# Chunked linear attention ahead of a gated matmul layer: from half-array matmuls on 128-token chunks to quarter-array matmuls on 64-token halves

## The chip, the cores and the metric

The kernel runs on one core of one Trainium2 chip. The metric is the device time of one execution in microseconds (us); smaller is better. Each kernel was run several times, and the medians below say of how many runs. "First output matmul" will mean the start of the first matmul that multiplies with `w_out`. It splits a run into a *start*, in which attention for the first four blocks has to wait for loads, and a *steady part*.

Engines are named as in the profile: PE is TensorE (matmuls), PEld its weight loads, DVE is VectorE, ACT is ScalarE, POOL is GpSimd (which in this kernel also issues most loads), SP is SyncE.

## The reference

```python
# q, k, v: (4 batches, 8 heads, 768 tokens, 64), float32
gamma = 1.0 - 2.0 ** (-5.0 - np.arange(8))
state = 0
for t in range(768):
    state = gamma * state + outer(k[t], v[t])          # per batch and head, 64x64
    y[t]  = (1/8) * q[t] @ state
x = y with the heads side by side                       # (3072, 512)
h = x @ w_in                                            # w_in (512, 2048)
out = (h * cos(h)) @ w_out                              # w_out (2048, 512), out (3072, 512)
```

The kernel works in bf16 with float32 accumulation. It removes gamma by scaling q with gamma^t/8 and k·v with gamma^-t, so that the recurrence becomes plain chunked attention: inside a chunk a masked score matrix (A) times V, plus q times the state at the start of the chunk; then the state grows by the chunk's K^T V.

## The kernel before

A "pair" is one chunk of 128 tokens of two batches, so there are 12 pairs, and two pairs make one group `g` of 512 columns of X. There are three attention stages per pair: scores and masks, Y (with the copy to X), and the state update. Around them TensorE does dense 128x128 matmuls: `unit_f` and `pair_f` multiply X with `w_in`, `unit_o` the activated result with `w_out`.

```python
# A: 16 matmuls, contraction 64, so two run side by side on the two row halves
def stage_a(p):
    for b in range(2):
        for a in range(HP):                 # HP = 4 couples of heads
            for j in range(2):              # head 2a+j
                nc.tensor.matmul(ap[j][:, a, :], lhsT=kt(n, b, a)[64*j : 64*j + 64, :],
                                 rhs=qt(n, b, a)[64*j : 64*j + 64, :], tile_position=(64*j, 0))
# Y: 32 matmuls with 64 output rows, two side by side on the column halves
def stage_yb(p, b):
    for a in range(HP):
        if c > 0:
            for j in range(2):              # q times state; stb holds zeros beside each 64x64 state
                nc.tensor.matmul(yp[ts(j, 64), a, :], lhsT=stb[p % 2][:, b, a, ts(j, 64)],
                                 rhs=qt(n, b, a), start=True, stop=False, ...)
        for j in range(2):                  # masked scores times V
            nc.tensor.matmul(yp[ts(j, 64), a, :], lhsT=vs[n][:, b, 2*a + j, :],
                             rhs=am[p % 2][b][j][:, a, :], ...)
    nc.scalar.copy(out=xt[(p // 2) % 2][:, :, ts(2 * (p % 2) + b, C)], in_=yp)
# S: 16 matmuls of 128x64, accumulated in one PSUM bank over all chunks of a batch
def stage_s(p, copy_st): ...
```

In the timeline of the kernel before, the two matmuls of a couple in A and in Y start 3 to 4 ns apart, and the next couple 56 ns after the first: about the time of 128 columns of one dense matmul (0.216 us for 512, so 54 ns). In that sense two run side by side.

A load of a part of `w_in` is one instruction on POOL. The part of the start that this text is about reads so (cuts marked by "..."):

```python
load(nc.gpsimd, 1, ("q0", "q1", "k0", "k1"))
load_w_in(0, 256); load_w_in(1, 256)
conv_q(1, nc.gpsimd)                         # POOL scales q of pair 1
load(nc.gpsimd, 1, ("v0", "v1")); load_w_in(1)
load(nc.gpsimd, 2, ("q0", "q1", "k0", "k1"))
conv_v(1, nc.gpsimd)                         # POOL scales v of pair 1
...
m1 = stage_a(1); masks(1, m1); pair_f(0, 0, (1,), later); ...
stage_y(1, nc.scalar.copy)                   # Y of both batches (each copied to X at once), then the state
pair_f(1, 0); pair_f(0, 1)                   # pair_f(p, r): r-th quarter of X(p) @ w_in
conv_q(2, nc.vector); conv_k(2, True); pair_f(1, 1); stage_t(2, None); ...
```

## Time and profile before

Before the change the median was 219.63 us of 3 runs (219.62 to 220.47).

| | before |
|---|---|
| span of the profiled run | 218.3 us |
| TensorE busy | 206.5 us, 95% |
| first output matmul | 58.09 us |
| from there to the end | 160.2 us |
| attention of one pair in the steady part, on TensorE | 2.0 us |

These lines are from the page of the kernel before. The first gives busy time, share of the span and number of instructions per engine; the next three are tenths of busy time in 40 slices of 5.5 us (PEclk is the clock that TensorE was granted, 9 being 90% or more); the last is the chain of waits that ended last, by engine.

```profile
PE 206.5 (95%) x1725; PEld 114.0 (52%) x1725; DVE 113.2 (52%) x183; ACT 118.4 (54%) x187; POOL 99.0 (45%) x113
...
PE   7986999989999999999999999999999999999993
...
POOL 7999999959999984729042070000000000000000
PEclk9999999999999999999999999999999999999999
...
PE 80%; POOL 9%; DVE 4%; ACT 4%; issue 2%; DVEq 0%; POOLq 0%; ACTq 0%
```

TensorE is the bound: from slice 10 to the last but one it is at 90% or more throughout. In the first fourteen slices POOL works with one gap, in slice 9, and it is the second engine of the chain of waits (9%). The granted clock is full in every slice of the row. But the trace has a record of the clock only from 6.54 us on; the ten dummy matmuls before, from 1.26 to 5.50 us, took 0.42 us each, twice the 0.216 us that a matmul of this size takes later. The same in microseconds, from the windows view of the kernel before (window, length, then busy time and number of instructions of PE, PEld, DVE, ACT, POOL; granted clock; DMA share; GB/s):

```profile
0.00:20.00 20.00, 16.11 (x143) 8.90 (x143) 12.35 (x29) 11.31 (x17) 18.82 (x27) 1.00 0.93 209
20.00:40.00 20.00, 18.10 (x244) 15.27 (x245) 14.12 (x23) 14.47 (x24) 19.87 (x24) 1.00 1.13 261
40.00:58.10 18.10, 16.62 (x206) 14.48 (x204) 13.65 (x22) 13.44 (x22) 15.72 (x18) 1.00 0.94 244
...
78.00:200.00 122.00, 122.00 (x866) 58.39 (x865) 64.25 (x97) 64.79 (x103) 24.76 (x26) 1.00 0.46 106
```

From 78 to 200 us TensorE never idles, and DVE and ACT are busy a little over half of the time. The waits view of the kernel before, TensorE from 8 us to the first output matmul (who waits for whom; us in total, times, longest):

```profile
PE bank_67 L234 <- POOL vs_119 L156: 1.6, 1, 1.6
...
PE bank_68 L292 <- ACT xt_135 L238: 0.5, 1, 0.5
PE bank_63 L292 <- ACT xt_134 L238: 0.4, 1, 0.4
...
PE bank_69 L234 <- POOL vs_119 L156: 0.4, 1, 0.4
```

All waits of that list, with those left out here, sum to 5.9 us. The longest is for `vs_119`, V of pair 1, which POOL scales. Waits for X (`xt`) after a Y stage are short, 0.4 to 0.5 us.

One Y stage with its state update, from the timeline of TensorE in the steady part (start, duration, engine, line, operation, output<-inputs, sizes, count):

```profile
137.58 1.03 PE L305 MATMUL bank_65<-w_out_sb,gt_136 128*128 128x512 bf16 x4
138.53 0.25 PE L229 MATMUL bank_64<-qkt_121,stb_133 128*64 128x128 bf16 x2
...
139.80 1.04 PE L281 MATMUL bank_66<-xt_135,w_in_sb 128*128 128x512 bf16 x4
```

Durations overlap (the page lists a dense matmul of 512 columns with 379 ns, while in the timeline they start 0.216 us apart), so starts are what to compare. Four dense matmuls of 512 columns take 0.86 us (0.216 each), so those that start at 137.58 are done at 138.45; the next dense one starts at 139.80. Y and the state cost 1.35 us, and A, in another place, 0.65: 2.0 us per pair. Each change between full and half array costs about 0.09 us of that, and there are four.

The first output matmul, from the same view of the start:

```profile
58.09 3.62 PE L305 MATMUL bank_66<-w_out_sb,gt_136 128*128 128x512 bf16 x16
```

### The profile page before, as it was taken

To read this page: it belongs to the slowest core of one execution; us is meant where nothing else is said; L and a number is where in the kernel's file an instruction comes from. 1 tells how busy PE (TensorE), PEld (TensorE's weight loads), DVE (VectorE), ACT (ScalarE), POOL (GpSimd) and SP (SyncE) were. 2 spreads that over 40 slices of the span, in tenths; PEclk is the share of its full clock that TensorE was granted. 3 is DMA by queue.
4 is the path that set the end of the run, shared out by engine and by line. 5 is a ranking of instruction groups with operands and counts; after the bars stand their busy time and mean duration, and the time that the engine had idled before them with its cause. 6 is when DMAs were issued, how large, how long until landed. Compare 5 with 4: busy or idle time off the path is not lost.

```text
span 218.3 us, 4318 instructions
## 1 busy us (share of the span) xinstructions
PE 206.5 (95%) x1725; PEld 114.0 (52%) x1725; DVE 113.2 (52%) x183; ACT 118.4 (54%) x187; POOL 99.0 (45%) x113
## 2 busy tenths in 40 slices
PE   7986999989999999999999999999999999999993
PEld 2554877968756454544544544544544544444441
DVE  4486496795714516557448537547647244433000
ACT  7365857848854656556456555555534634444120
POOL 7999999959999984729042070000000000000000
PEclk9999999999999999999999999999999999999999
DMA  6999999999476999792991942613511011110212
GB/s 156 324 161 235 264 282 236 203 305 332 116 241 164 291 223 290 182 296 54 182 250 55 158 127 82 66 48 99 51 48 51 0 48 48 51 48 2 96 62 82
DMA packets 44084, 32.78 MB, mean 150 GB/s; under 512 B 32800, under 2 KB 37664, under 8 KB 44064
## 3 DMA queue, kind: packets, MB, share of 16 engines
q0 software_dynamic: 9072, 18.35, 33.4%
q1 hardware_dynamic: 34848, 14.03, 27.6%
q8 instruction: 13, 0.21, 0.4%
q10 hardware_dynamic: 144, 0.13, 0.2%
q14 instruction: 7, 0.06, 0.1%
HBM read 27.26 MB, written 6.29 MB: 154 GB/s over the span
## 4 chain that ended last, share of the span: by engine, by line
PE 80%; POOL 9%; DVE 4%; ACT 4%; issue 2%; DVEq 0%; POOLq 0%; ACTq 0%
PE bank_65 L305 10%; PE bank_63 L281 9%; PE bank_67 L305 8%; PE bank_68 L305 6%; PE bank_66 L305 6%; PE bank_64 L281 5%; PE bank_69 L281 4%; PE bank_69 L305 4%; PE bank_66 L281 4%; PE bank_67 L281 3%; PE bank_63 L292 2%; PE bank_64 L292 2%; PE bank_63 L305 2%; PE bank_64 L305 2%; POOL qs_113 L151 1%
## 5 line engine op out<-in xcount | busy, mean ns | idle before, releaser
L281 PEld LDWEIGHTS <-w_in_sb 128*128 128x128 bf16 x256 | 24.1, 98 | 28.3
L305 PEld LDWEIGHTS <-gt_137 128*128 128x128 bf16 x192 | 18.8, 98 | 22.7
L305 PEld LDWEIGHTS <-gt_136 128*128 128x128 bf16 x192 | 18.5, 98 | 21.6
L292 PEld LDWEIGHTS <-w_in_sb 128*128 128x128 bf16 x256 | 24.6, 98 | 4.0 <-issue 0.9
L305 PE MATMUL bank_67<-w_out_sb,gt_136 128*128 128x512 bf16 x64 | 16.3, 379 | 0.0
L305 PE MATMUL bank_65<-w_out_sb,gt_136 128*128 128x512 bf16 x64 | 16.1, 379 | 0.0
L281 PE MATMUL bank_63<-xt_134,w_in_sb 128*128 128x512 bf16 x48 | 12.4, 380 | 0.0
L305 PE MATMUL bank_66<-w_out_sb,gt_137 128*128 128x512 bf16 x48 | 11.8, 379 | 0.0
L305 PE MATMUL bank_68<-w_out_sb,gt_137 128*128 128x512 bf16 x48 | 11.8, 379 | 0.0
L263 ACT ACTIVATE cosb_140<-bank_63,halfpi 128x512 bf16<-128x512 f32 x10 | 6.9, 688 | 7.3 <-PE bank_63 L281 6.4
L327 PE MATMUL bank_63<-gt_137 128*128 128x512 bf16 x29 | 9.1, 470 | 1.3 <-DVE gt_137 L130 1.3
L263 ACT ACTIVATE cosb_139<-bank_63,halfpi 128x512 bf16<-128x512 f32 x9 | 6.2, 688 | 7.5 <-PE bank_63 L281 6.5
L263 ACT ACTIVATE cosb_138<-bank_63,halfpi 128x512 bf16<-128x512 f32 x8 | 5.5, 688 | 7.7 <-PE bank_63 L281 7.5
L281 PE MATMUL bank_63<-xt_135,w_in_sb 128*128 128x512 bf16 x36 | 9.3, 380 | 0.0
L281 PE MATMUL bank_64<-xt_134,w_in_sb 128*128 128x512 bf16 x32 | 8.2, 380 | 0.0
L305 PE MATMUL bank_69<-w_out_sb,gt_137 128*128 128x512 bf16 x32 | 8.2, 379 | 0.0
L305 PE MATMUL bank_65<-w_out_sb,gt_137 128*128 128x512 bf16 x32 | 8.2, 379 | 0.0
L255 DVE CAST stb_133<-st_ps 64x512 bf16<-64x512 f32 x8 | 5.5, 689 | 5.0 <-PE st_ps L250 4.8
L312 DVE COPY ob_111<-bank_68 128x256 f32<-128x256 f32 x1 | 0.4, 425 | 13.3 <-PE bank_68 L305 13.3
L263 ACT ACTIVATE cosb_140<-bank_64,halfpi 128x512 bf16<-128x512 f32 x7 | 4.8, 688 | 4.6 <-PE bank_64 L281 3.0
L281 PE MATMUL bank_69<-xt_135,w_in_sb 128*128 128x512 bf16 x28 | 7.2, 379 | 0.0
L281 PE MATMUL bank_66<-xt_135,w_in_sb 128*128 128x512 bf16 x28 | 7.2, 379 | 0.0
(399 smaller groups left out, 501.4 us busy)
## 6 DMA issues: line engine op xcount, KB each, us to landing
w_out_sb<-in_moe_w_out_dram POOLq DMA_DIRECT2D x4, 512.0 KB, 9.9
w_in_sb<-in_moe_w_in_dram POOLq DMA_DIRECT2D x3, 512.0 KB, 7.5
out_dram<-ob_108 SPq DMA_DIRECT2D x6, 256.0 KB, 2.2
out_dram<-ob_109 SPq DMA_DIRECT2D x6, 256.0 KB, 2.0
out_dram<-ob_110 SPq DMA_DIRECT2D x6, 256.0 KB, 2.1
out_dram<-ob_111 SPq DMA_DIRECT2D x5, 256.0 KB, 2.0
kf_1_89<-in_k_dram POOLq DMA_DIRECT2D x3, 256.0 KB, 5.0
vf_1_99<-in_v_dram POOLq DMA_DIRECT2D x3, 256.0 KB, 5.1
```

Source lines behind the costliest of these rows:

```text
L151: eng.tensor_tensor(out=qs[p % NB][:, b], in0=qf[p % PRE][b], in1=bc(gq, p % NC), op=ALU.mult)
L255: copy_st(out=stb[(p + 1) % 2][ts(j, 64), :, :, ts(j, 64)], in_=st_ps[ts(j, 64)])
L263: nc.scalar.activation(out=cb, in_=bank, func=AF.Sin, bias=halfpi)
L281: nc.tensor.matmul(bank, lhsT=w_in_sb[:, i, ts(f, 128)], rhs=xt[g % 2][:, i, :], start=(i == 0), stop=(i == KIN - 1))
L292: nc.tensor.matmul(bank[:, ts(e, 256)], lhsT=w_in_sb[:, i, ts(f + e, 128)], rhs=xt[g % 2][:, i, ts(hf, 256)], start=(i == 0 and e == 0), s ...
L305: nc.tensor.matmul(bank, lhsT=gt[g % 2][:, f, ts(j, 128)], rhs=w_out_sb[:, f, :], start=(f == 0), stop=(f == KOUT - 1))
L312: nc.vector.tensor_copy(out=o[:, ts(0, 256)], in_=bank[:, ts(0, 256)])
L327: nc.tensor.matmul(spare, lhsT=zero[:, :128], rhs=zero, start=True, stop=True, skip_group_check=True)
```

## The change

The intent: a 64x64 quarter is the natural size of every attention matmul here if a chunk is cut into two halves of 64 tokens. Of the masked score matrix the upper right quarter is zero, and what the lower left one carries now goes through the state after the first half, so neither is computed; the zeros beside the states are gone; and four matmuls are to run at once. All of it for two neighbouring pairs goes into one block (Y of one pair, A and state of the next), so that the array changes its tiling twice per pair instead of four times.

```diff
-    am = ... [128, HP, 128] per batch and head       mask [128, 128]
+    am = [[sb([128, 2, HP, 64], BF16, ...) for r in range(2)] for i in range(2)]
+    stf = sb([128, 2, 2 * HP * D], FP32, "stf")      # state after each half, kept in SBUF
+    mask = sb([128, 64], BF16, "mask")
 ...
     def load_w_in(r, n=512):
+        src = moe_w_in[:, ts(r, n)].rearrange("(x m p) f -> p x m f", m=4, p=64)
+        dst = w_in_sb[:, :, ts(r, n)].rearrange("p (x y) f -> p x y f", y=2)
         nc.gpsimd.dma_start(
-            out=w_in_sb[:, :, ts(r, n)],
-            in_=moe_w_in[:, ts(r, n)].rearrange("(i p) f -> p i f", p=128))
+            out=dst[:, :, 0],
+            in_=moe_w_in[:, ts(r, n)].rearrange("(x y p) f -> p x y f", y=2, p=128)[:, :, 0])
+        for hh in range(2):
+            nc.gpsimd.dma_start(out=dst[ts(hh, 64), :, 1], in_=src[:, :, 3 - hh])
 ...
+    def block(py=None, pa=None, pu=None):
+        ...                                   # mm(bank, col, cols, row, ...) = one 64x64 quarter (row, col)
+        if py is not None:                    # q times the state at the start of each half u
+            ...  mm(yb[u, r], j ^ r, ts(2*b + x, 64), j, st[...], qt(n, b, a)[half(j), half(u)])
+        if pa is not None:                    # scores of the next pair, inside each half u only
+            ...  mm(yb[b, j ^ u], u, ts(4 + a, 64), j, kt(...)[half(j), half(u)], qt(...)[half(j), half(u)])
+        if pu is not None:                    # K^T V of each half of the next pair
+            ...  mm(bank, j, ts(4*b + a, 64), u, ks[n][half(u), ...], vs[n][half(u), ...])
+        if py is not None:
+            nc.tensor.drain()                 # the next matmuls add to the same PSUM from other array rows
+            ...  mm(yb[u, r], j ^ r, ts(2*b + a//2, 64), u, vs[...], am[...])
+        ...                                   # DVE: four masks; ACT: four copies to X, 128x256 each
+        if pu is not None:
+            for u, bank in enumerate(ub):     # DVE adds to the float32 state, ACT casts it to bf16
+                nc.vector.tensor_tensor(out=stf[:, u], in0=bank, in1=stf[:, 1 - u], op=ALU.add)
+                nc.scalar.copy(out=stb[pu % 2][:, u], in_=stf[:, u])
 ...
-    load(nc.gpsimd, 2, ("q0", "q1", "k0", "k1"))
+    load(nc.gpsimd, 2, ("q0", "q1"))
     conv_v(1, nc.gpsimd)
+    load(nc.gpsimd, 2, ("k0", "k1"))
 ...
-    stage_y(1, nc.scalar.copy)
+    block(pu=1)
+    pair_f(0, 1)
+    block(py=1)
     pair_f(1, 0)
-    pair_f(0, 1)
     conv_q(2, nc.vector)
 ...
-    m2 = stage_a(2); masks(2, m2)
+    block(pa=2)
     pair_f(1, 2)
-    stage_y(2, nc.scalar.copy)
+    block(pu=2)
     pair_f(0, 3)
+    block(py=2)
 ...
-    m3 = stage_a(3); masks(3, m3)
+    block(pa=3, pu=3)
     pair_f(2, 2, (1,)); pair_f(2, 3)
-    stage_y(3, nc.scalar.copy)
+    block(py=3)
     for r in range(4): pair_f(3, r)
 ...
+    plan = {g: [(5, "b", 2*g + 2), (5, "c", 2*g + 4), (13, "b", 2*g + 3), (13, "c", 2*g + 5)] ...}
+    # "b": block(py=p, pa=p+1, pu=p+1)     "c": scale q, k, v of pair p and transpose q and k
```

Y of an odd couple of heads comes out with its two heads swapped (`j ^ r`), so the rows of X are permuted, and to match them each load of `w_in` becomes three loads. And the copies to X come after the whole block instead of after each batch.

## The prediction

One cut took a term out of the sum for a full block: the author's estimate for the explicit drain. The two terms that are left come to 1.06 + 0.18 = 1.24 us; with the term the sum was the 1.4 us that stands there, and the 4.2 us saved and the 217.9 us in all were reckoned with it.

> **What bounds the kernel now.** TensorE. The page has PE busy 95% of 218.3 us, at full granted clock in every slice; the chain of waits is 80% PE, 9% POOL. From 80 to 200 us (windows view) PE never idles, while DVE and ACT are busy 54% and 53%. Before 60 us the start is paced by POOL and the loads: in the timeline POOL works without a pause to 44 us, and TensorE waits 1.7 us for POOL's scaled V of pair 1, which is ready only at 21.3 us.
>
> **What attention costs TensorE now (timeline, starts of single matmuls, steady state).** A of a pair: 8 row-tiled couples at 56 ns = 0.45 us. Y: 16 column-tiled couples at 56 ns = 0.89 us. State: 8 couples with N=64 at 31 ns = 0.25 us. Each change of tiling (full to quarter or back) costs about 90 ns over the normal spacing; there are four per pair.[...] Between the dense matmuls A takes 0.65 us and Y with state 1.35 us: 2.0 us per pair.
>
> **What the change does there.** 128 matmuls of 64x64 with N=64 per pair, in rounds of four on different quarters. The state couples show 31 ns for N=64, and neighbouring instructions issue 2 ns apart, so eight instructions per round are not the limit. Estimate: 32 rounds at 33 ns = 1.06 us, two switches 0.18[...]: 1.4 us for a full block, 0.9 for Y alone, 0.75 for A with state. From pair 4 on this saves about 4.2 us, all on the critical path.
>
> **What it costs.** At the start (to about 60 us):
> - Each w_in load becomes three POOL loads. POOL loads take 0.75 to 0.80 us with 512 pieces and 0.9 with 1024, so mostly fixed; estimate 2.0 instead of 0.77 us, +6 us of POOL for the five. Moving two K loads behind the scaling of V(1) gives 1.8 back: V(1) ready near 23.3 instead of 21.3, V(2) near 38 instead of 32. TensorE will wait for both.
> - The four copies to X start only after the whole Y block, then pair_f needs them at once (pairs 0, 1, 3): about 1.5 us of wait instead of 0.5, each.
> - Pairs 0 to 2 have separate blocks, so little array gain.
> Sum: 2 to 4 us lost before the first output group; I take 2.5. DVE has smaller masks but new float32 state adds; ACT has four X copies and two state copies per pair. Neither reaches its limit in the steady state, and eight banks suffice.
>
> **Time.** 219.6 - 4.2 + 2.5 = 217.9, so 217.9 us; range 213.5 to 222.5. Faster by over 2%: 0.22; within 2%: 0.68; slower: 0.10.
>
> **What would show each step.** Timeline of a steady block: spacing of rounds near 33 ns, whole gap between dense matmuls 1.3 to 1.5 us. Waits: TensorE on POOL's V of pairs 1 and 2, and on ACT's X copies, in the first 60 us. DMA issues: each part of w_in near 0.65 us of POOL. First output-projection matmul later than the 58.1 us of now, by 2 to 4 us; from there to the end shorter by about 4 us.
>
> **What would make it wrong.** Quarters that do not run four at a time (rounds at 60 ns: about 12 us slower in all); a drain of 0.5 us;[...] ACT or DVE tails after a block that hold banks or X; or half-width loads that cost POOL in proportion to their size, which gives the start back and 215 us.

## More of the kernel before

`warm(n)` issues n dummy matmuls of 512 columns, where TensorE would otherwise idle at the very beginning.

Before 58 us TensorE idles 3.4 us of the last 38.

## The result, and the profile after

The changed kernel took **226.88 us** (median of 4 runs, 226.62 to 227.58); the kernel before, run beside it, 220.05 us (median of 4, 219.62 to 221.43). The ratio is 1.0304 (95% interval 1.0249 to 1.036): slower by 3%, and outside the predicted range. Ratios here and below are the mean time of one kernel's fast runs over the mean of the other's fast runs of the same rounds, so they are not quite the ratio of the medians quoted. The output is correct.

| | before | after |
|---|---|---|
| span of the profiled run | 218.3 | 225.4 |
| TensorE busy | 206.5 | 205.8 |
| first output matmul | 58.09 | 67.29 |
| from there to the end | 160.2 | 158.1 |

So the start lost 9.2 us and the steady part gained 2.1. The page of the kernel after, same rows as above:

```profile
PE 205.8 (91%) x2491; PEld 111.9 (50%) x2491; DVE 103.9 (46%) x191; ACT 125.8 (56%) x225; POOL 104.1 (46%) x124
...
PE   7954679897599999999999999999999999999993
...
PEclk9998599999699999999999999999999999999999
...
PE 76%; POOL 7%; DVE 5%; ACT 4%; DMA 3%; issue 2%; DVEq 0%; ACTq 0%; POOLq 0%
```

Two holes have opened in the PE row, at slices 3 to 6 and at slices 10 and 11, and in the PEclk row slices 4, 5 and 11 fall to 8, 5 and 6: for a part of them TensorE was granted half its clock (0.50 in the windows view further down). The DMA engines are new in the chain of waits, with 3%. The windows view of the kernel after:

```profile
0.00:20.00 20.00, 15.31 (x219) 8.32 (x220) 9.72 (x30) 11.09 (x19) 18.70 (x31) 1.00 0.85 190
20.00:40.00 20.00, 14.71 (x258) 11.23 (x258) 10.80 (x20) 9.92 (x18) 18.00 (x23) 0.83 1.02 230
40.00:67.30 27.30, 23.06 (x369) 18.95 (x368) 18.11 (x31) 17.86 (x34) 25.64 (x29) 0.94 0.96 228
...
86.40:207.00 120.60, 119.76 (x1261) 56.85 (x1250) 57.99 (x98) 71.08 (x128) 22.75 (x24) 1.00 0.43 108
```

In the steady stretch, DVE works less (58.0 against 64.3) and ACT more (71.1 against 64.8), and neither limits. From 20 us to the first output matmul TensorE idles 9.5 us (20.00 - 14.71 + 27.30 - 23.06) where it idled 3.4 before. Counted from the beginning, TensorE is busy for 53.08 of the first 67.3 us and was busy for 50.83 of the first 58.1: of the 9.2 us lost, about 7.0 are more idle time and 2.2 are more busy time; some of its matmuls ran slower, as shown below.

The first output matmul, timeline of TensorE in the kernel after:

```profile
67.29 3.62 PE L335 MATMUL bank_66<-w_out_sb,gt_133 128*128 128x512 bf16 x16
```

**The start: waits.** The waits view of the kernel after, TensorE from 8 us to the first output matmul:

```profile
PE bank_69 L218 <- POOL vs_119 L161: 3.1, 2, 2.5
PE bank_66 L322 <- ACT xt_132 L270: 2.3, 1, 2.3
PE bank_64 L322 <- DMA w_in_sb<-in_moe_w_in_dram: 1.8, 2, 1.5
PE bank_65 L178 <- POOL qs_113 L156: 1.6, 1, 1.6
PE bank_69 L322 <- ACT xt_131 L270: 1.0, 1, 1.0
...
PE bank_66 L218 <- ACT stb_129 L285: 0.7, 1, 0.7
PE bank_70 L322 <- ACT xt_131 L270: 0.6, 1, 0.6
```

All listed waits sum to 12.6 us, 6.7 more than before. Three kinds grew or are new. POOL's scaled q and V: 4.7 instead of 2.0. X after a block: 3.9 instead of 0.9. `w_in` itself: 1.8 instead of nothing, because `pair_f(0, 1)` was moved ahead and the loads became slower. A fourth is small and had been overlooked: the second half of a pair's Y needs the state after the first half of the same pair, so Y now waits for matmul, DVE add (0.69 us) and ACT cast (0.62) of the state (`stb_129`, 0.7).

Why POOL is late, in the timeline of POOL, first of the kernel before, then of the kernel after (one load of a part of `w_in`):

```profile
14.87 0.80 POOL L115 DMA_DIRECT2D w_in_sb<-in_moe_w_in_dram  x1
```

```profile
16.51 0.74 POOL L118 DMA_DIRECT2D w_in_sb<-in_moe_w_in_dram  x1
17.20 1.25 POOL L122 DMA_DIRECT2D w_in_sb<-in_moe_w_in_dram  x2
```

The same bytes occupy POOL 2.0 instead of 0.8 us: an issue costs nearly the same whether it moves a half (0.74 us) or a quarter of the part (1.25 for two). This is as predicted.

Why X is late, in the timeline of ACT in the kernel after, behind the Y block of pair 3, whose last matmul starts at 56.34 us:

```profile
57.24 0.69 ACT L293 ACTIVATE cosb_137<-bank_68,halfpi 128x512 bf16<-128x512 f32 x1
57.81 0.38 ACT L270 CAST xt_132<-bank_69 128x256 bf16<-128x256 f32 x1
...
```

ACT is busy with two casts of the state until 56.2, then with the three cosines that stand ahead in its queue, and only then makes the four copies of 0.38 to 0.42 us; TensorE stands until 58.79.

**The start: the clock.** The windows view of the kernel after, cut at the moments at which the granted clock changed (the third number from the end is the clock):

```profile
17.52:20.93 3.41, 1.38 (x41) 1.09 (x41) 2.61 (x6) 1.37 (x2) 3.41 (x5) 1.00 0.97 152
20.93:24.34 3.41, 1.25 (x33) 0.69 (x32) 1.38 (x2) 0.62 (x1) 3.41 (x5) 0.50 1.07 239
24.34:27.75 3.41, 2.71 (x13) 1.90 (x14) 0.30 (x1) 1.30 (x2) 3.41 (x6) 0.50 0.94 217
55.06:58.47 3.41, 1.34 (x69) 0.98 (x68) 2.14 (x4) 3.23 (x8) 3.39 (x5) 1.00 1.04 346
58.47:61.88 3.41, 3.09 (x15) 2.06 (x15) 0.64 (x2) 1.23 (x3) 3.41 (x4) 0.50 0.91 299
```

Ahead of each drop lies a stretch of 3.41 us in which TensorE was busy for 1.38 and 1.34 us only. After it the clock is half for 6.83 and for 3.41 us. The two drops are eleven times 3.41 us apart (58.47 - 20.93 = 37.54), and the two of e7 (below) 26 times (108.59 - 19.84 = 88.75), so in these profiles the stretches lie on a fixed grid. What it costs is seen in the timeline of TensorE in the kernel after:

```profile
25.05 1.65 PE L322 MATMUL bank_64<-xt_131,w_in_sb 128*128 128x256 bf16 x7 [1.53 <-DMA w_in_sb<-in_moe_w_in_dram]
26.49 1.66 PE L322 MATMUL bank_65<-xt_131,w_in_sb 128*128 128x256 bf16 x8
...
66.42 1.04 PE L322 MATMUL bank_65<-xt_132,w_in_sb 128*128 128x256 bf16 x8
```

Eight matmuls of 256 columns take 0.87 us at full clock (66.42 to the first output matmul at 67.29); seven take 1.44 at half clock (25.05 to 26.49). Half of the busy time in the three half-clock stretches, (1.25 + 2.71 + 3.09)/2 = 3.5 us, is an estimate of what the clock cost. It is rather too high: where TensorE would have waited anyway, slower matmuls cost nothing. The four runs of the changed kernel themselves show no such cost. Their mean granted clock was 0.970 and 0.985 in two runs that both took 226.62 us, and 0.977 in the two of 227.15 and 227.58; estimated back from these means, about four, two and three stretches of 3.41 us at half clock.

**The steady part: a block.** The timeline of TensorE in the kernel after, one full block:

```profile
128.71 1.03 PE L335 MATMUL bank_69<-w_out_sb,gt_133 128*128 128x512 bf16 x4
129.67 0.22 PE L218 MATMUL bank_67<-qkt_123,stb_130 64*64 64x64 bf16 x2
...
130.47 0.19 PE L218 MATMUL bank_66<-vs_118,ks_115 64*64 64x64 bf16 x1
130.78 0.21 PE L218 MATMUL bank_67<-am_0_124,vs_120 64*64 64x64 bf16 x1
...
131.16 1.04 PE L311 MATMUL bank_65<-xt_132,w_in_sb 128*128 128x512 bf16 x4
```

The dense matmuls before are done at 129.57 (128.71 + 4 x 0.216), the next starts at 131.16: 1.59 us for a block, against 2.0 before. The 24 rounds of four between 129.67 and 130.47 take 33 ns each, and 64 columns of one dense matmul alone take 27 (0.216 us / 8), so four quarters do run at once. The pause between 130.47 and 130.78 is the explicit drain: 0.31 us, 0.28 more than a normal round.

### The profile page after: what moved, and what is told of

It reads as the page before. It is cut to its first block, busy times and chain, and to the rows that moved or that the text cites. A ratio compares the mean times of both kernels' runs of the same rounds, so it can differ in the third digit from the quotient of the medians.

```text
span 225.4 us, 5875 instructions
## 1 busy us (share of the span) xinstructions
PE 205.8 (91%) x2491; PEld 111.9 (50%) x2491; DVE 103.9 (46%) x191; ACT 125.8 (56%) x225; POOL 104.1 (46%) x124
## 4 chain that ended last, share of the span: by engine, by line
PE 76%; POOL 7%; DVE 5%; ACT 4%; DMA 3%; issue 2%; DVEq 0%; ACTq 0%; POOLq 0%
PE bank_68 L335 9%; PE bank_70 L335 7%; PE bank_66 L335 5%; PE bank_67 L335 5%; PE bank_69 L335 4%; PE bank_69 L311 4%; PE bank_66 L311 4%; PE bank_64 L311 4%; PE bank_65 L311 3%; PE bank_63 L311 3%; PE bank_67 L311 3%; DMA w_in_sb<-in_moe_w_in_dram 3%; PE bank_63 L335 3%; PE bank_68 L311 2%; PE bank_70 L311 2%
## 5 line engine op out<-in xcount | busy, mean ns | idle before, releaser
L311 PEld LDWEIGHTS <-w_in_sb 128*128 128x128 bf16 x256 | 24.5, 98 | 29.1 <-issue 0.5
L322 PEld LDWEIGHTS <-w_in_sb 128*128 128x128 bf16 x256 | 25.7, 103 | 11.3 <-issue 4.5
L335 PE MATMUL bank_68<-w_out_sb,gt_134 128*128 128x512 bf16 x48 | 12.3, 379 | 0.0
L335 PE MATMUL bank_70<-w_out_sb,gt_133 128*128 128x512 bf16 x48 | 12.2, 379 | 0.0
L335 PE MATMUL bank_69<-w_out_sb,gt_133 128*128 128x512 bf16 x48 | 12.0, 379 | 0.0
L335 PE MATMUL bank_68<-w_out_sb,gt_133 128*128 128x512 bf16 x48 | 12.0, 380 | 0.0
L285 ACT CAST stb_130<-stf 128x512 bf16<-128x512 f32 x10 | 6.2, 618 | 8.6 <-DVE stf L282 8.4
L285 ACT CAST stb_129<-stf 128x512 bf16<-128x512 f32 x12 | 7.3, 617 | 5.6 <-DVE stf L282 3.4
L335 PE MATMUL bank_67<-w_out_sb,gt_134 128*128 128x512 bf16 x32 | 7.7, 379 | 0.0
L335 PE MATMUL bank_70<-w_out_sb,gt_134 128*128 128x512 bf16 x32 | 7.7, 379 | 0.0
L335 PE MATMUL bank_63<-w_out_sb,gt_134 128*128 128x512 bf16 x32 | 7.7, 379 | 0.0
L335 PE MATMUL bank_66<-w_out_sb,gt_134 128*128 128x512 bf16 x32 | 7.7, 379 | 0.0
L293 ACT ACTIVATE cosb_136<-bank_65,halfpi 128x512 bf16<-128x512 f32 x8 | 5.5, 685 | 3.6 <-PE bank_65 L311 3.4
L293 ACT ACTIVATE cosb_136<-bank_69,halfpi 128x512 bf16<-128x512 f32 x8 | 5.5, 690 | 3.5 <-PE bank_69 L311 2.2
L293 ACT ACTIVATE cosb_137<-bank_63,halfpi 128x512 bf16<-128x512 f32 x8 | 5.5, 689 | 3.1 <-PE bank_63 L311 2.6
L311 PE MATMUL bank_69<-xt_131,w_in_sb 128*128 128x512 bf16 x28 | 7.2, 380 | 0.0
L300 DVE TENSOR_TENSOR gt_133<-bank_69,cosb_136 128x512 bf16<-128x512 f32 x5 | 3.5, 692 | 8.0 <-ACT cosb_136 L293 8.0
L122 POOL DMA_DIRECT2D w_in_sb<-in_moe_w_in_dram x10 | 6.3, 676 | 0.0
```

The lines of the kernel that those rows point to most:

```text
L122: nc.gpsimd.dma_start(out=dst[ts(hh, 64), :, 1], in_=src[:, :, 3 - hh])
L285: nc.scalar.copy(out=stb[pu % 2][:, u], in_=stf[:, u])
L293: nc.scalar.activation(out=cb, in_=bank, func=AF.Sin, bias=halfpi)
L300: nc.vector.tensor_tensor(out=out, in0=h, in1=cb, op=ALU.mult)
L311: nc.tensor.matmul(bank, lhsT=w_in_sb[:, i, ts(f, 128)], rhs=xt[g % 2][:, i, :], start=(i == 0), stop=(i == KIN - 1))
L322: nc.tensor.matmul(bank[:, ts(e, 256)], lhsT=w_in_sb[:, i, ts(f + e, 128)], rhs=xt[g % 2][:, i, ts(hf, 256)], start=(i == 0 and e == 0), s ...
```

## The experiments

Three suspects for the loss at the start stood at first. *The loads* (called theory L): three issues per part hold up POOL. *The clock* (theory C): the waits only trigger it, and the half clock is what costs. And *the blocks* of the new start: X after a whole block, the state within a pair. All times are medians; "before" is the kernel before in the same rounds. A range is that of all runs of the kernel; a run is called slow if it is over 1.5% above the fastest of its kernel, and ratios use fast runs only. "Wrong" means that the result is not the reference's, while the work is the same in kind and amount.

| run | median us | ratio to before, interval | first output matmul |
|---|---|---|---|
| changed kernel | 226.88 | 1.0304, 1.0249 to 1.036 | 67.29 |
| e1 plain `w_in` loads, wrong | 226.98 | 1.0309, 1.0238 to 1.038 | 67.00 |
| e2 before with split loads | 224.17 | 1.0197, 1.0087 to 1.0307 | 62.81 |
| e3 changed, 21 dummy matmuls | 223.92 | 1.0176, 1.0103 to 1.0249 | 63.90 |
| e4 old start, quarters from pair 4, split loads | 222.06 | 1.008, 1.0012 to 1.0148 | 61.92 |
| e5 changed, dense work behind the block of pair 3 | 225.13 | 1.0084, 0.9932 to 1.0237 | slow profile |
| e6 old start, old loads, quarters from pair 4, wrong | 218.59 | 0.9865, 0.9733 to 0.9997 | 57.92 |
| e7 as e6, made correct | 218.26 | 0.9865, 0.9763 to 0.9966 | slow profile |
| e8 as e1, V of pair 2 later, wrong | 225.38 | 1.0213, 1.0087 to 1.0339 | 63.27 |
| e9 before, 7 dummy matmuls | 222.36 | 1.0001, 0.9932 to 1.007 | slow profile |
| e10 as e7, 12 dummy matmuls | 218.88 | 0.990, 0.9844 to 0.9956 | 58.58 |
| e11 changed, 40 dummy matmuls | 225.36 | 1.0203, 1.015 to 1.0257 | 64.67 |
| e12 as e10, conversions ahead of the block | **217.83** | 0.9899, 0.9864 to 0.9935 | 58.10 |
| e13 as e11, conversions ahead of the block | 224.74 | 1.0218, 1.0175 to 1.0261 | 64.26 |

### e1: the changed kernel with one load per part of w_in

```diff
     def load_w_in(r, n=512):
-        src = ...; dst = ...
         nc.gpsimd.dma_start(
-            out=dst[:, :, 0], in_=...[:, :, 0])
-        for hh in range(2):
-            nc.gpsimd.dma_start(out=dst[ts(hh, 64), :, 1], in_=src[:, :, 3 - hh])
+            out=w_in_sb[:, :, ts(r, n)],
+            in_=moe_w_in[:, ts(r, n)].rearrange("(i p) f -> p i f", p=128))
```

The result is wrong: the rows of `w_in` no longer match those of X.

> The changed kernel with each part of w_in loaded by one POOL load again, as in the kernel before; nothing else is changed (the result is wrong on purpose: the rows of two slices are not swapped). Theory L (the split loads make most of the late start): the last piece of the second w_in part lands about 2 us earlier, TensorE does not fall to the half clock in the first window, first output-projection matmul at 61 to 63 us instead of 67.3, total 220 to 222.5 us. Rival S (the order of the new blocks at the start, with late X copies and a state needed within the pair, makes most of it): first output matmul at 65.5 or later, total 225 to 226.5 us.

It took 226.98 us (226.14 to 228.0): nothing gained, so the loads alone are not the cause, or the gain is given back. At least a part was given back. The step `pair_f(1, 0)` started at 27.91 us instead of 30.10, but then V of pair 2, which POOL reached earlier, was scaled at the same time as DVE scaled q of pair 2, in the timelines of DVE and POOL of e1:

```profile
31.34 2.89 DVE L151 TENSOR_TENSOR qs<-qf,gq 128x512 bf16<-128x512 f32 x2
```

```profile
32.16 2.98 POOL L156 TENSOR_TENSOR vs<-vf,gk 128x512 bf16<-128x512 f32 x2
```

DVE needs 1.45 us a piece here, and 0.64 without the collision (e8 below); TensorE waited 1.9 us for that q, in two waits. POOL needs 1.49 a piece here, and 1.04 to 1.14 for V in the kernel after. Two pieces of DVE at 0.64 and two of POOL at about 1.1 would make 3.5 us one after the other, and the four together took 3.8 (31.34 to 35.14): in time it is as if the two engines had taken turns. What makes them do so was not shown. The clock dropped twice in this profile, too, at 22.08 and 59.62, for 3.41 us each.

### e2: the kernel before with the loads split in three

```diff
     def load_w_in(r, n=512):
+        src = ...; dst = ...                      # as in the change
         nc.gpsimd.dma_start(
-            out=w_in_sb[:, :, ts(r, n)], in_=...)
+            out=dst[:, :, 0], in_=...[:, :, 0])
+        for hh in range(2):
+            nc.gpsimd.dma_start(out=dst[ts(hh, 64), :, 1], in_=src[:, :, 2 + hh])
```

Here the rows are not permuted, so the result is correct.

> The kernel before with each part of w_in loaded in three POOL loads, one of 128 and two of 64 partitions, rows in their own order, so the result is right; nothing else is changed. Theory L: 3 us or more slower than the kernel before, 223 to 226 us, first output matmul at 61.5 to 64 us. Rival S: at most 1.5 us slower, 220 to 221.5 us.

It took 224.17 us (223.45 to 226.57), and the first output matmul came 4.7 us later than before (62.81 against 58.09). So the split loads do cost as expected when they are added alone. But the profile shows how, in the waits of TensorE and in the windows view of e2:

```profile
PE bank L238 <- POOL vs L160: 4.3, 1, 4.3
```

```profile
22.40:29.30 6.90, 6.25 (x65) 4.95 (x66) 0.69 (x1) 3.18 (x6) 6.90 (x11) 0.51 0.97 213
```

The wait for V of pair 1 grew from 2.0 to 4.3 us, and behind it TensorE ran at half clock for 6.83 us. Half of the 6.25 us of busy time is 3.1 us: an estimate, but larger than the 2.3 us by which the wait grew. Time and first output matmul are as theory L expected; that the slower clock makes a part of them is read from the profile.

### e3: the changed kernel with dummy matmuls in two waits

```diff
+    spare = banks.take(); warm(11); banks.give(spare)
     block(pu=1)
 ...
     block(py=3)
+    spare = banks.take(); warm(10); banks.give(spare)
     for r in range(4):
```

Nothing is taken away here: TensorE only works instead of waiting, at two places.

> The changed kernel with dummy matmuls (11 and 10 of N=512) put where TensorE only waits: before the state block of pair 1 and after the Y block of pair 3. Theory C (the half clock after idle time, 6.8 us from 20.9 and 3.4 us from 58.5, costs by itself): granted clock 1.00 through the start, first output matmul 2 to 3.5 us earlier (64 to 65.3), total 223.5 to 225 us. If the half clock only covers time that is waited anyway: 226.3 to 227.5 us.

It took 223.92 us (223.27 to 225.31): 3.0 us less than the changed kernel, from adding useless work. This is what theory C expected, and nothing that theory L explains. One drop of 3.41 us remained in the profile, at 15.30. Two things stay open. The dummies also take a PSUM bank and give it back, so that later tiles use other banks; no run tested this apart. And of the four runs the one of 225.31 us had a mean clock of 0.977, as much half clock as the profiled run of the changed kernel, and was still faster than every run of the changed kernel (226.62 and up).

### e4: the old start with the new loads, quarters from pair 4 on

```diff
-    block(pa=0)
+    m0 = old_a(0); old_masks(0, m0)
 ...
-    block(pu=1); pair_f(0, 1); block(py=1); pair_f(1, 0)
+    old_y(1); pair_f(1, 0); pair_f(0, 1)
 ...                                              # likewise for pairs 2 and 3
+    # old_s(3) hands its state over: nc.vector.tensor_copy(out=stf[:, 1], in_=st_bank), cast to stb
```

The `old_*` stages are those of the kernel before with the swapped head order.

> The changed kernel with pairs 0 to 3 by the full and half array matmuls, the tiles and the order of the kernel before, and quarters only from pair 4 on; the loads stay those of the change (split w_in, moved K loads); the result is right. Rival S: first output matmul back at 58.5 to 60.5 us, total 218 to 219.5 us. Theory L: first output matmul at 62 us or later, total 221 us or more.

It took 222.06 us (221.05 to 222.78), as theory L expected, and the first output matmul came at 61.92, just ahead of what theory L expected and later than S allowed. Of the 9.2 us lost at the start, the loads with their drop of the clock (here one, of 3.41 us) carry 3.8, and the new blocks with their own waits and drops carry the other 5.4. This split holds for this order of taking away; seen from the changed kernel, plain loads gain less (e1 nothing, e8 1.5 us in the medians).

### e5: dense work in the wait behind the block of pair 3

```diff
     block(py=3)
+    for i in range(3):
+        unit_o(0, 0, i)                          # 12 dense matmuls that come later otherwise
     for r in range(4):
         pair_f(3, r)
```

> The changed kernel with three quarters of the first output tile's work (12 matmuls, 2.6 us) moved between the Y block of pair 3 and the projection that waits for its X copies; nothing is added. If the wait for X and the half clock after it are the loss there: no half-clock window near 58 us, total 3 to 4 us less, 222.8 to 224 us. If that wait only hides another one: 226 to 227 us.

The four runs: 222.98 and 223.14 us (fast), and 227.11 and 227.7 (slow). The fast ones are as expected, but two runs are few, and the interval, 0.9932 to 1.0237, leaves it unclear. The profile is of a slow run, with a half clock of 10.24 us from 23.77 on; it does show the wait for X at pair 3 gone: the twelve dense matmuls start at 58.48 and, at 0.216 us each, end at 61.07, and `pair_f` starts at 61.08. So this run supports the mechanism of that wait, and gives no usable size.

### e6: old start and old loads, quarters from pair 4 on

```diff
 (as e4, and)
-    three-part load_w_in
+    one load per part
-    load(nc.gpsimd, 2, ("q0", "q1")); conv_v(1, nc.gpsimd); load(nc.gpsimd, 2, ("k0", "k1"))
+    load(nc.gpsimd, 2, ("q0", "q1", "k0", "k1")); conv_v(1, nc.gpsimd)
```

Wrong, as e1.

> Pairs 0 to 3 by the scheme of the kernel before and its loads of w_in and K in its order, quarters from pair 4 on (the result is wrong on purpose: two slices of w_in are not swapped). If start and steady state add up (5.4 us for the blocks of the start and 3.8 us for the loads, both measured at the first output matmul): first output matmul at 58 to 59 us, total 217.3 to 218.8 us, 2 us under the kernel before. If the steady state of the quarters were the loser: 221 us or more.

The fast runs took 217.44, 217.62 and 219.56 us, one slow run 222.74; the ratio of the fast runs is 0.9865. The profile had full clock throughout. With the old start the first output matmul is back at the time of before (57.92 against 58.09), and from there to the end it takes 158.0 us, as the changed kernel does. So start and steady part add up, and the whole of the loss is in the start.

### e7: the same, correct

The permutation of X can be taken out of `w_in`: the heads of the second batch are loaded in reverse order for q and k, and the two batches of one head couple then fill the four quarters.

```diff
-                in_=src[2*bp + b, :, ds(c*C, C)].rearrange("h t d -> t h d"))
+                in_=(src[2*bp + b, ::-1] if b and n[0] != "v" else src[2*bp + b])[
+                    :, ds(c*C, C)].rearrange("h t d -> t h d"))
 ...
-                            mm(yb[u, r], j ^ r, ts(2*b + x, 64), j, ...)
+                            mm(yb[u, b], COL(b, a, j), ts(SLOT(b, a), 64), j, ...)   # COL = j ^ b
```

> The same, made right without touching w_in: q and k of the second batch are loaded with their heads in reverse order, so that their odd heads lie on the lower rows, and the four quarters of a round come from the two batches. Result right; time within 0.7 us of the run with the old start and plain loads, so 217.3 to 219 us and faster than both kernels. If reversed loads cost DMA or POOL time: above 220 us.

The fast runs took 218.07, 218.16 and 218.37 us, ratio 0.9865; a slow one, which was profiled, 221.62. That profile shows a second place at which the clock can drop, far from the start, in the waits of TensorE after 66 us:

```profile
PE bank L306 <- DMA qkt<-ks: 1.6, 1, 1.6
```

The transposes of k of pair 8 by DMA came late; TensorE waited 1.6 us, and from 108.59 to 112.00 it ran at half clock. ACT copied the source behind the casts of the block, but that is not the whole cause: in e10, with the same order, ACT copied it at the same time (98.28 us, here 98.09) and no wait followed. The transposes themselves took 8.0 us from issue to landing here and 4.8 in e10. Why is open. (A first drop, of 3.41 us at 19.84, lies in the start.)

### e8: e1 with V of pair 2 scaled later

```diff
-    conv_v(2, nc.gpsimd)
     for r in range(4):
         load_w_out(r)
+    conv_v(2, nc.gpsimd)
```

> The run with plain loads of w_in and the new start, with POOL's scaling of V of pair 2 moved behind its four w_out loads (result wrong on purpose, as there). There VectorE's scaling of q of pair 2 took 1.45 us a piece instead of 0.69, at the same time as POOL's scaling of V. Theory: the two engines slow each other, and this gave back what plain loads gained: 0.69 us a piece now, TensorE's transposes of pair 2 no longer wait, first output matmul 1.0 to 1.8 us earlier than 67.0, total 225 to 226 us. If not: 0.69 does not come back, or 226.5 to 227.5 us.

It took 225.38 us (223.13 to 226.97), as expected, and the first output matmul came at 63.27, much earlier than expected; the profiled run is the fastest of the four. The collision of e1 is confirmed; the timeline of DVE in e8:

```profile
30.40 1.28 DVE L151 TENSOR_TENSOR qs<-qf,gq 128x512 bf16<-128x512 f32 x2
```

Each piece takes 0.64 us again. But this profile had only one drop of the clock (16.97, 3.41 us) where e1 had two, so the size of the collision's part cannot be told from that of the clock.

### e9: the kernel before with dummy matmuls in its longest wait

```diff
+    spare = banks.take(); warm(7); banks.give(spare)
     stage_y(1, nc.scalar.copy)
```

The kernel before has runs of up to 225.5 us among those of 219.05, and the question was whether its wait of 1.6 us causes them.

> The kernel before with 7 dummy matmuls of N=512 where TensorE waits for the scaled V of pair 1. Runs of the kernel before spread from 219.4 to 225.1 us on the last chip. Theory C (that spread, too, is half clock after this wait, in steps of one 3.4 us window): all runs of this kernel within 1 us of 219.6, none at 222 to 225. If the spread has another cause: the same spread as the kernel before in the same rounds.

It did not. Fast runs took 219.57 to 221.81 us (ratio 1.0001), and 222.92 and 223.00 still came, at a mean clock of 0.992 and 0.991. One run, 308.04 us, had a mean granted clock of 0.658 from beginning to end; it is a slow run and enters no ratio. What makes single runs of the kernel before slower is open. One lead: in the rounds of the experiments, the six runs of the kernel before at 224.8 us or more all had a mean clock of 0.985, by estimate two stretches of 3.41 us at half clock, and all those below 219.7 had 0.997 or more. No trace of a slow one was kept, so neither what lowers the clock nor whether that is the cause is shown.

### e10: e7 with dummy matmuls in two waits

```diff
     old_s(0)
+    spare = banks.take(); warm(5); banks.give(spare)
     pair_f(0, 0, (0,), later)
 ...
+    spare = banks.take(); warm(7); banks.give(spare)
     old_y(1)
```

> The run with old start, plain loads and reversed heads, with 7 and 5 dummy matmuls in its two waits of the first 20 us; result right. Theory: no half-clock window after 15 us, runs at 217.0 to 218.3 us with little spread, about 2 us (0.9%) under the fast runs of the kernel before. If dummy matmuls get in the way: 219 us or more.

The fast runs took 217.45, 217.63, 218.36 and 219.41 us, and two slow ones 222.89 and 222.96 (clock 0.992 and 0.991). The ratio of the fast runs is 0.990. The spread is a miss: the dummies at the start did not rid the kernel of slow runs.

### e11: the changed kernel with dummy matmuls in all its waits

```diff
+    warm(6), warm(3), warm(11), warm(5), warm(5), warm(10)   # in six waits between 12 and 58 us
```

> The changed kernel with dummy matmuls in all its longer waits up to 58 us (six places, 40 matmuls), loads and order as they are. Theory C with idle: the clock is full from 15 us on, and what stays against the kernel before is waiting alone: 222.0 to 223.8 us, 3 to 4 us under the changed kernel. If half clock only falls on time that is waited anyway: 226 us or more.

It took 225.36 us (five fast runs, 224.41 to 225.97; one slow, 229.92), where 222 to 223.8 had been expected: a miss. The profile had full clock throughout, and still the first output matmul came at 64.67, 6.6 us later than before. So the clock is not the larger part of the loss. Part of the miss is a new wait of 1.45 us, from 111.9 to 113.4, for the transposes of pair 8, as in e7; they took 7.7 us here.

### e12: e10 with the conversions ahead of the block

```diff
-    plan = {g: [(5, "b", 2*g + 2), (5, "c", 2*g + 4), (13, "b", 2*g + 3), (13, "c", 2*g + 5)] ...}
+    plan = {g: [(5, "c", 2*g + 4), (5, "b", 2*g + 2), (13, "c", 2*g + 5), (13, "b", 2*g + 3)] ...}
```

ACT thereby copies k of the next pair, on which the transposes depend, ahead of the X copies and state casts of the block.

> The mended version (old start, plain loads, reversed heads, dummies in the first two waits) with the conversions and DMA transposes of a pair put ahead of the block of the same step instead of behind it. In a slow profile of the mended version TensorE waited 1.8 us at about 105 us for the transposed k of pair 8, whose k copy stood behind the block's X and state copies on ACT, and then ran one window at half clock. Theory: that wait is gone, the runs lie at 217 to 218.3 us with fewer at 222 to 223, ratio to the kernel before 0.985 to 0.991. If the slow runs have another cause: as many of them as before, two or three in six.

It has the lowest median: 217.83 us (fast runs 217.61 to 218.4, one slow run 221.28), ratio 0.9899 with the interval 0.9864 to 0.9935, so 1% faster than the kernel before, and correct. Against e10 (ratio 0.990) the new order gained nothing that could be measured: the wait for the transposes of pair 8 is not among its waits, but it is not among those of e10 either, and one slow run in six against two is too few to tell. The clock of its profile is full in every slice, and its span is 216.2 us. Its first output matmul in the timeline of TensorE:

```profile
58.10 3.62 PE L418 MATMUL bank<-w_out_sb,gt 128*128 128x512 bf16 x15
```

The start is that of before, and the rest takes 216.2 - 58.1 = 158.1 us, 2.1 less than before. A second profiled run of the same kernel agrees: span 215.9, first output matmul at 57.85, the rest 158.0 us. What is left of the change, when the start is left alone, is what the quarters save in the steady part.

### e13: e11 with the conversions ahead of the block

```diff
-    plan = {g: [(5, "b", 2*g + 2), (5, "c", 2*g + 4), ...
+    plan = {g: [(5, "c", 2*g + 4), (5, "b", 2*g + 2), ...        # as in e12
```

> The changed kernel with dummies in all longer waits of the start, and the conversions ahead of the blocks. Theory: clock 1.00 and no wait for transposes, first output matmul still near 64.7 us, total 222.3 to 223.3 us: of the 6.8 us that the change cost, some 3 are waits at the start and 4 half clock. If the half clock is not worth 3 to 4 us: 224 us or more.

It took 224.74 us (six fast runs, 223.84 to 225.56), again above the 222.3 to 223.3 expected, and so on the side named for "the half clock is not worth 3 to 4 us". The first output matmul came at 64.26 with a clock of 0.998 (64.48 in a second profiled run), the rest took 158.1 us. With a full clock the changed kernel still is 6.2 us late at the start; the changed kernel itself is 9.2 late. So filling the waits, and with it the full clock, is worth about 3.0 us in the profiled run (67.29 - 64.26), or 2.1 in the medians (226.88 - 224.74), less than the estimate of 3.5. That all of it is the clock is argued, not shown: the dummies may cost something themselves where they outlast a wait, and they change the order of the PSUM banks; neither was measured apart.

## Why the prediction was wrong

The direction of both terms was right and their sizes were not. The prediction was 219.6 - 4.2 + 2.5; measured in the two profiles it is 218.3 - 2.1 + 9.2 = 225.4.

- **"2 to 4 us lost before the first output group; I take 2.5."** This is the step that failed. The start lost 9.2 us, some 7.0 of it more idle time of TensorE and 2.2 more busy time. E6 and e12 show that this is all of the loss: with the old start it is gone.
  - *The waits were named, but not added up.* POOL's q and V cost 2.7 us more (4.7 against 2.0), X 3.0 more (3.9 against 0.9): 5.7 from causes that the prediction itself lists (though 1.6 of it is for the scaled q of pair 1, where it named only V of pairs 1 and 2, and no wait for V of pair 2 appears), among them "about 1.5 us of wait instead of 0.5, each" for three pairs, which alone is 3. Taking 2.5 for the sum had no ground.
  - *Two waits were missed.* `w_in` in DMA, 1.8 us, because `pair_f(0, 1)` comes earlier while the loads come later; and the state inside a pair, 0.7 us.
  - *The clock is in no term.* The prediction read the row PEclk of before, full in every slice, as if it were a given. In the profile of the changed kernel TensorE fell to half clock for 10.2 us in all. Filling the waits with useless matmuls, with a mean clock of 0.992 (e3), 1.0 (e11) and 0.998 (e13) in the profiles instead of 0.977, gained 1.5 to 3.0 us (medians of e3, e11 and e13 against the changed kernel).
- **"Moving two K loads behind the scaling of V(1) gives 1.8 back: V(1) ready near 23.3 instead of 21.3, V(2) near 38 instead of 32."** About right: 22.3 and 39.1.
- **"Each w_in load becomes three POOL loads ... estimate 2.0 instead of 0.77 us."** Right: 2.0.
- **"Rounds of four at 33 ns."** Right, 31 to 33 ns.
- **"1.4 us for a full block."** Too small: 1.59. Its term for the explicit drain (cut above) was the author's estimate and too small as well: 0.28 measured. A full block therefore saves 0.4 us and not 0.6; with six full blocks from pair 4 on that is 2.5 us where the prediction counted 3.6. The other blocks, for which it counted 0.6, gained nothing, by difference (2.1 in all).
- **"From pair 4 on this saves about 4.2 us, all on the critical path."** It saved 2.1, and all of it on the critical path: e6 and e12 keep the same 158 us from the first output matmul on.
- **"Neither reaches its limit in the steady state."** Right, ACT was busy 71.1 of 120.6 us and DVE 58.0.
- **"ACT or DVE tails after a block that hold banks or X"** was named as what could make it wrong. It did, in the start only.

What is shown: the loss lies in the start (e4, e6, e12), and the loads and the new blocks each carry a part (e2, e4). That the clock carries a part within both is likely (e3, e11, e13) but not free of a rival, the changed order of banks, and the single runs of the changed kernel do not follow their clock. What is not settled: the split in microseconds. The drops of the clock fall in different places from kernel to kernel (once or twice, 3.41 to 10.24 us), so that e1 and e8, which differ from the changed kernel by little, do not give clean differences. Roughly, e4 puts 3.8 of the 9.2 us on the loads and 5.4 on the blocks, both with their drops of the clock; e13 puts up to 3 of the same 9.2 on the clock. It is also open why single runs of the kernel before are 2 to 6 us slower.

What lay ahead of the drops can be counted. Over the eleven drops in the profiles of the changed kernel and of e1 to e8, TensorE was busy for 0.0 to 1.68 us of the 3.41 us ahead ten times, and for 1.95 once (e3). Two stretches that kept their clock come close to that: one of 1.77 us in the changed kernel (10.69 to 14.10), and the emptiest of the start of the kernel before, 1.94 us, in its windows view:

```profile
16.78:20.19 3.41, 1.94 (x29) 1.26 (x26) 2.82 (x5) 1.77 (x3) 3.41 (x5) 1.00 1.11 195
```

So in this measure the stretches with and without a drop behind them overlap, between 1.77 and 1.95 us, and the start of the kernel before is close to a drop. That busy time is what decides is read from these stretches, not tested by a run of its own.

## What to carry to other kernels

A change that speeds up the steady part should leave the start alone until the steady gain has been measured by itself: here the old start with the new steady part is 1% faster than before, and the complete change 3% slower. In a start that is short of loads, count what each issue costs the engine that issues it (here 0.62 to 0.80 us of POOL for one load of `w_in`), add up every wait that you can name instead of guessing their sum, and look for moved steps that need data earlier than before. And treat TensorE's clock as something that the schedule can lower: add up its busy time over stretches of the length seen here, 3.41 us. Here ten of eleven drops to half clock came after a stretch with at most 1.68 us of busy time; by estimate from these (3.41 - 1.68) a wait of some 1.7 us inside one stretch could be enough.
